# A third buffer for split keys, a second for split queries, weights staged in x's third buffer, and a new order

## The chip, the core and the metric

The kernel runs on one core of a Trainium2 chip. The metric is the device time of one execution in microseconds (us). The engines are TensorE (PE, with its weight loads PEld), VectorE (DVE), ScalarE (ACT), GpSimd (POOL) and SyncE (SP), whose queue issues all the DMAs of this kernel.

## What is computed

An attention with pooled queries feeds a channel mix (inputs: q, k, v of 8 batches, 8 heads, 1152 positions, 64 channels):

```
q_pool = q.reshape(B, H, S // 2, 2, D).mean(axis=3)          # 576 queries
attn   = softmax(scale * q_pool @ k^T)                       # over 1152 keys
x      = (attn @ v), heads side by side                      # (8, 576, 512)
x_prev = x shifted by one position
xk = mu_k * x + (1 - mu_k) * x_prev;  xr = mu_r * x + (1 - mu_r) * x_prev
out = sigmoid(xr @ w_r) * (relu(xk @ w_k)**2 @ w_v)          # 512 -> 1024 -> 512
```

## The kernel before

Everything is 16-bit on PE, in pairs of a high and a low part, so most products are made two or three times. The 64 heads (batch by batch) are gone through in blocks of 96 queries, six a head, 384 in all.

**A block** (function `block`): PE multiplies the nine chunks of keys ks1 with the queries qT (line 544), DVE takes the maximum mx over the chunks (551), PE turns it (554), DVE takes the maximum mb over the partitions (556), PE brings it back as a row (558), ACT writes that row into the low queries (561, qT), PE adds the low parts ks2 with the row (567), and ACT takes the exponentials pf (573). POOL makes their low part pl (581). Three PSUM tiles s are in turn, so up to three blocks are on the way.

**The output** (`window`, `halves`): four or five windows of 128 queries a head (631, 633, 638), and one pair of half windows for two heads (602), summed in the PSUM bank a, divided on DVE, turned (667), and put into xt (678), one of three buffers by batch.

**The feed-forward** (`mix`, `ff`): tiles of 256 rows of x, as soon as a batch is done; all its products stand in line 839, in the PSUM bank f. They fill PE between the blocks of the next batch; what is left over runs after the last block.

**Preparing a head** (`prep`, `queries`): loads of k, v (kr, vr, two buffers each) and of q for two heads (qr, qs, one buffer). Keys are split into high (ACT, line 489) and low (DVE, 492) in kn, **two buffers**. A DMA transpose (499) turns kn into ks1 (two buffers), and a DMA (501) copies its upper half into ks2. The queries of two heads are split in the same way (ACT 441, DVE 445) in qn, **one buffer**, and turned by two DMA transposes (456). So the split of a head's keys waits until the transpose of the head two before has landed, which itself can be issued when PE has done the last scores with that ks1. The heads 0 and 1 are turned on PE (466).

**The weights** (`weights`): 20 pieces of 512 KB are loaded into two staging buffers st (696), decoded from 64-bit numbers by ACT (707 into the bank f, and 716), DVE (719), rounded by ACT (721), with POOL making the low part (722).

**The order**: every operation goes into a list with an engine, a duration, what it reads and writes, and a key (class `Issue`). `run` plays that list through a small model several times (`play`, `follow`), shifts priorities by the numbers in MOVES, and writes the instructions of each engine in the order of the model's start times. Each engine works strictly in that order. LATE, SLACK, SEED and MOVES, and the durations and loads at each `op`, only act through this order.

Of the kernel before, what the change touches and what calls it, by code (L numbers as in the profile page):

```python
# [11 lines left out]
F32 = mybir.dt.float32  # L12
F16 = mybir.dt.float16
BF16 = mybir.dt.bfloat16
I32 = mybir.dt.int32
# [6 lines left out]
P = 128  # L22
# [23 lines left out]
W_FIRST, W_STEP, W_REST, W_REST_STEP = 3.0, 2.0, 32.0, 2.5  # L46
# [3 lines left out]
LATE, SLACK = 0.04, 0.05  # L50
# [6 lines left out]
PE_T = 2  # L57
WDEP = [("ks1", 1), ("ks2", 0), ("vr", 1)]
AHEAD2 = 0
MOVES, BASE, REACH = (  # L60
# [7 lines left out]
SEED, SPREAD = 2, 5.0  # L68


class Issue:
# [15 lines left out]
    def add(self, eng, dur, fn, r=(), w=(), key=0.0, port=None, load=0.0):  # L87
# [23 lines left out]
        self.ops.append((eng, dur, fn, key, deps, eng == "POOL" if port is None else port, None, (dur, load)))  # L111
# [117 lines left out]
    def graph(self, late, slack):  # L229
        ops = self.ops  # L230
        eng = [o[0] for o in ops]
        dur = [o[1] * (1.0 if o[0] in ("PE", "DMA") else 1.0 + late) for o in ops]
        load = [o[7][1] * (1.0 + late) if o[0] == "DMA" else 0.0 for o in ops]
        pred, succ, back = ([[] for _ in ops] for _ in range(3))
        for n, o in enumerate(ops):
            for m, lat in o[4].items():
                more = slack if eng[m] != eng[n] or eng[n] == "DMA" else 0.0
                succ[m].append((n, lat + more))
                pred[n].append(m)
                back[n].append((m, (self.ISSUED + self.LANDED if eng[m] == "DMA" else lat) + more))  # L240
        return (eng, dur, [o[5] for o in ops], load), succ, pred, back
# [54 lines left out]
def kernel(  # L296
# [64 lines left out]
    kn = bufs("kn", 2, [P, NC, P], F16)  # L361
    qn = bufs("qn", 1, [P, 2, NQ, P], F16)
# [15 lines left out]
    sg = bufs("sg", 2, [P, DM], F16)  # L378
# [23 lines left out]
    nc.gpsimd.memset(qn[0][:, 1, :, 0:D], 0.0)  # L402
# [9 lines left out]
    for t_ in xt:  # L412
        nc.vector.memset(t_[:, :, 0:1], 0.0)


    def queries(n, key):

        b, h = divmod(n, H)
        i = n // 2 % 2
# [13 lines left out]
        for j0, j1 in JS:  # L433
            js, jk = slice(j0, j1), range(j0, j1)
            for nj, ck, o_, src in pieces(j0, j1):
                op("DMA", 0.45, lambda o_=o_, src=src: nc.sync.dma_start(o_, src), w=ck,
                   key=key - 2 * NB * PER, load=0.27 * nj + 0.05)
# [3 lines left out]
            op("ACT", (j1 - j0) * P / 1200 + 0.093, lambda js=js, j1=j1, j0=j0: nc.scalar.activation(  # L441
                qn[0][:, 0, js].rearrange("p j (r d) -> p j r d", r=2),
                qs[0][:, js].unsqueeze(2).broadcast_to([P, j1 - j0, 2, D]), AF.Copy, scale=SQ),
               r=[("qs", c) for c in jk], w=[("qn", c) for c in jk], key=key + 1)
            op("DVE", (j1 - j0) * D / 960 + 0.069, lambda js=js: nc.vector.scalar_tensor_tensor(
                qn[0][:, 1, js, D:P], qs[0][:, js], SQ, qn[0][:, 0, js, 0:D], op0=ALU.mult, op1=ALU.subtract),
               r=[("qs", c) for c in jk] + [("qn", c) for c in jk], w=[("qnl", c) for c in jk], key=key + 2, port=True)

        for j0, j1 in JS if n < PE_T else ((0, NQ),):
            js, jk = slice(j0, j1), range(j0, j1)  # L450
            for r_, m, t_, bank, kb, eng in ((0, "qn", "qT", a_b, ("a",), "ACT"), (1, "qnl", "qTl", f_b, ("f",), "DVE")):
                if n < PE_T and j0 < 5:
                    turn16([qn[0][:, r_, c] for c in jk], bank, kb, [(m, c) for c in jk],
                           qT[i][:, r_, js], [(t_, i, c) for c in jk], eng, key + 2)
# [22 lines left out]
    def prep(n, key):  # L477

        b, h = divmod(n, H)
        i, j = n % 2, n % NV  # L480
        def dma(o, src, buf):
            op("DMA", 0.42, lambda: nc.sync.dma_start(o, src), w=[buf], key=key - 2 * NB * PER, load=1.21)
# [3 lines left out]
        for c0, c1 in ((0, 5), (5, NC)):  # L486
            cs = slice(c0, c1)
            nn = (c1 - c0) * D
            op("ACT", nn / 1200 + 0.093, lambda cs=cs: nc.scalar.copy(kn[i][:, cs, 0:D], kr[i][:, cs]),
               r=[("kr", i)], w=[("kn", i, c0)], key=key)  # L490
            e, en, d = ("POOL", nc.gpsimd, nn * 0.0022 + 0.1) if n < KN_POOL else ("DVE", nc.vector, nn / 960 + 0.069)
            op(e, d, lambda cs=cs, en=en: en.tensor_tensor(
                kn[i][:, cs, D:P], kr[i][:, cs], kn[i][:, cs, 0:D], op=ALU.subtract),
               r=[("kr", i), ("kn", i, c0)], w=[("knl", i, c0)], key=key + 1, port=True)
        if n < PE_T:
            turn16([kn[i][:, c] for c in range(NC)], s_b[2], ("s", 2), [(x, i, c) for x in ("kn", "knl") for c in (0, 5)],
                   None, None, (("ACT", 0, 5, ks1[i][:, 0:5], [("ks1", i)]), ("DVE", 5, NC, ks1[i][:, 5:NC], [("ks1", i, 5)])), key + 1)
# [3 lines left out]
        op("DMA", 0.54, lambda: nc.sync.dma_start(ks2[i][D:P], ks1[i][0:D]),  # L501
           r=[("ks1", i), ("ks1", i, 5)], w=[("ks2", i)], key=key + 1, load=0.9)
# [115 lines left out]
    def window(n, w, t):  # L618
# [45 lines left out]
        for t0, t1 in TURN:  # L664
# [7 lines left out]
            for y, (q0, q1) in enumerate(SPAN):  # L672
                if (y < 3) != (t0 == 0):
# [6 lines left out]
                   r=[ka], w=[("xt", b % 3, g, y)], key=t + O_TURN)  # L680


    def weights(n, w, kc, key, step):
        cols = w.shape[1]
        wv = w.bitcast(I32).rearrange("(c p) (f t) -> c p f t", p=P, t=2)
        for c in range(kc):
            for f in range(0, cols, 512):
# [9 lines left out]
                   r=WDEP if iss.nw <= 2 else [], w=[ks], key=key, load=2.41)  # L697
# [5 lines left out]
                mi, km, sz, kz = m_.bitcast(I32), ("em", i), sg[i], ("sg", i)  # L703
# [63 lines left out]
                if dec == "P":  # L767
                    op("ACT", 0.565, lambda sz=sz, wh=wh: nc.scalar.activation(sz, wh.bitcast(F32), AF.Sign),
                       r=[ks], w=[kz], key=key)
                    op("POOL", 1.24, lambda e=e, sz=sz: nc.gpsimd.tensor_tensor(e, e, sz, op=ALU.mult),  # L770
                       r=[ke, kz], w=[ke], key=key)
                else:
                    v_(0.6, lambda ei=ei, wh=wh: nc.vector.scalar_tensor_tensor(
                        ei, wh, -0x80000000, ei, op0=ALU.bitwise_and, op1=ALU.bitwise_or), [ks, ke], [ke])
# [142 lines left out]
    weights("v", w_v, NF, (W_REST + 4 * W_REST_STEP) * PER, W_REST_STEP * PER)  # L917
    tiles = [(t, min(t + T, B * TQ)) for t in range(0, B * TQ, T)]
# [66 lines left out]
```

## Time and profile before

| | |
|---|---|
| median of 3 runs | 1143.21 us (1142.04 to 1145.67) |
| profiled execution | 1141.87 us, span 1140.1 us |
| granted TensorE clock | 1.000 of full speed (2.4 GHz) |
| busy: PE, DVE, ACT, POOL | 1091.6, 921.2, 846.6, 519.5 us |
| chain that ended last | PE 65%, DMA 7%, DVE 3%, ACT 2% |
| of it, by line | L839 26% (bank f), keys' transposes 6%, queries' 2% |

The span runs from the first to the last instruction. Matmul rows are pipelined: each is about 0.2 us long, and the next starts well before its end, so PE's busy time holds more than work. Idle time is shown ahead of the instruction that ended it, with what released it.

### The profile page before, as it was taken

How to read it: one execution, taken by the hardware profiler on the slowest of the kernel's cores; microseconds unless marked ns; L12 is line 12 of the kernel's file. 1: busy time of each engine (PE TensorE's matmuls, PEld its weight loads, DVE VectorE, ACT ScalarE, POOL GpSimd, SP SyncE). 2: the span in 40 equal slices, each digit the busy share in tenths (PEclk: the TensorE clock that was granted, in tenths of full speed). 3: DMA queues.
4: the chain of work that ended last, by engine and by line, in shares of the span. 5: the costliest groups of instructions: out<-in, count | busy, mean ns of one | idle time of the engine just before them, and what ended most of it. 6: DMA issues, size and time to landing. Idle time of an engine off the chain costs nothing.

```text
span 1140.1 us, 44737 instructions
## 1 busy us (share of the span) xinstructions
PE 1091.6 (96%) x18956; PEld 894.1 (78%) x18956; DVE 921.2 (81%) x1860; ACT 846.6 (74%) x1915; POOL 519.5 (46%) x573
## 2 busy tenths in 40 slices
PE   6888899999999999999999999999999999999998
PEld 5777878878787878878786978888787878887565
DVE  8999899988989788789877888797888887874431
ACT  7899987778677786777767676777777686765643
POOL 2566745545454444545353544445353544543111
PEclk9999999999999999999999999999999999999999
DMA  7998576554545555663454553564445534310000
GB/s 204 245 223 186 136 164 126 120 131 98 117 107 125 117 109 116 116 123 80 117 117 79 127 106 96 98 141 107 93 112 107 108 93 86 74 28 11 20 19 28
DMA packets 218745, 125.71 MB, mean 110 GB/s; under 512 B 154032, under 2 KB 190896, under 8 KB 218544
## 3 DMA queue, kind: packets, MB, share of 16 engines
q1 hardware_dynamic: 218544, 122.86, 49.0%
q8 instruction: 148, 2.42, 0.9%
q14 instruction: 53, 0.43, 0.1%
HBM read 67.11 MB, written 9.44 MB: 67 GB/s over the span
## 4 chain that ended last, share of the span: by engine, by line
PE 65%; DMA 7%; DVE 3%; ACT 2%; issue 1%; SPq 0%; ACTq 0%; DVEq 0%
PE f L839 26%; PE s L544 8%; PE s L567 8%; DMA ks<-kn 6%; PE s L839 4%; PE a L638 4%; PE a L633 4%; PE a L631 4%; DMA qT<-qn 2%; PE a L839 2%; PE a L602 1%; PE s L554 1%; PE a L667 1%; PE s L558 1%; DVE mx L551 1%
## 5 line engine op out<-in xcount | busy, mean ns | idle before, releaser
L581 POOL TENSOR_SCALAR pl<-pf 128x864 f16<-128x864 uint16 x384 | 368.8, 960 | 434.3 <-ACT pf L573 404.1
L551 DVE TENSOR_REDUCE mx<-s 128x96 f16<-128x864 f32 x384 | 399.8, 1053 | 84.5 <-PE s L544 55.9
L573 ACT ACTIVATE pf<-s 128x864 int32<-128x864 f32 x384 | 333.6, 883 | 73.6 <-PE s L567 55.6
L544 PE MATMUL s<-qT,ks 128*128 128x96 f16 x3456 | 220.9, 207 | 12.7 <-ACT pf L573 11.4
L567 PE MATMUL s<-qT,ks 128*128 128x96 f16 x3456 | 216.4, 206 | 11.4 <-ACT qT L561 10.6
L544 PEld LDWEIGHTS <-ks 128*128 128x128 f16 x3456 | 183.8, 98 | 40.6 <-issue 16.5
L567 PEld LDWEIGHTS <-ks 128*128 128x128 f16 x3456 | 180.2, 98 | 32.6 <-issue 15.1
L633 PE MATMUL a<-vt,pf 128*128 128x64 f16 x2304 | 192.8, 194 | 0.0
L631 PE MATMUL a<-vt,pf 128*128 128x65 f16 x2304 | 192.4, 193 | 0.3 <-ACT xt L678 0.2
L631 PEld LDWEIGHTS <-pf 128*128 128x128 f16 x2304 | 162.4, 99 | 4.6
L633 PEld LDWEIGHTS <-pf 128*128 128x128 f16 x2304 | 155.6, 97 | 6.3 <-issue 0.5
L561 ACT ACTIVATE qT<-s 1x96 f16<-1x96 f32 x384 | 87.5, 232 | 86.0 <-PE s L558 79.5
L839 PE MATMUL f<-xhk,wk_hi 128*128 128x256 f16 x496 | 135.2, 273 | 0.1
L839 PE MATMUL f<-xhk,wk_lo 128*128 128x256 f16 x496 | 135.2, 273 | 0.0
L839 PE MATMUL f<-xlk,wk_hi 128*128 128x256 f16 x496 | 135.2, 273 | 0.0
L556 DVE TENSOR_REDUCE mb<-s 128x1 f16<-128x128 f32 x384 | 109.4, 287 | 25.6 <-PE s L554 21.7
L638 PE MATMUL a<-vb,pl 128*128 128x65 f16 x2304 | 122.6, 193 | 0.4 <-issue 0.4
L870 POOL TENSOR_TENSOR gl<-g 128x512 f16<-128x512 f32 x72 | 76.5, 1062 | 95.9 <-ACT g L868 93.5
L839 PEld LDWEIGHTS <-wk_hi 128*128 128x128 f16 x1152 | 106.0, 98 | 11.5 <-issue 0.2
L638 PEld LDWEIGHTS <-pl 128*128 128x128 f16 x2304 | 96.7, 98 | 5.5 <-issue 0.5
L839 PE MATMUL f<-wv_hi,g 128*128 128x512 f16 x240 | 90.9, 379 | 0.3 <-ACT em L889 0.3
L839 PE MATMUL f<-wv_lo,g 128*128 128x512 f16 x240 | 90.9, 379 | 0.0
(110 smaller groups left out, 2032.2 us busy)
## 6 DMA issues: line engine op xcount, KB each, us to landing
kr<-in_k_dram SPq DMA_DIRECT2D x64, 288.0 KB
vr<-in_v_dram SPq DMA_DIRECT2D x64, 288.0 KB
qr<-in_q_dram SPq DMA_DIRECT2D x63, 256.0 KB
ks<-ks SPq DMA_DIRECT2D x64, 144.0 KB
out_dram<-em SPq DMA_DIRECT2D x36, 256.0 KB
st<-in_moe_w_k_dram SPq DMA_DIRECT2D x8, 512.0 KB
st<-in_moe_w_v_dram SPq DMA_DIRECT2D x8, 512.0 KB
qr<-in_q_dram SPq DMA_DIRECT2D x32, 64.0 KB
```

The source lines that it names most:

```text
L544: nc.tensor.matmul(cols(c, c + 1), ks1[hp][:, c, :], qhi, start=(c == c0), stop=False, skip_group_check=True)
L551: op("DVE", 0.975, lambda: nc.vector.tensor_reduce(mxz[:, P - QN:P], grid(0, NC).rearrange("p c q -> p q c"), axis=AX.X, op=ALU.max), r=[( ...
L556: op("DVE", 0.199, lambda: nc.vector.tensor_reduce(mbz, s[:, 0:P], axis=AX.X, op=ALU.max), r=[("s", z)], w=[("mb", z)], key=t + O_MAX)
L561: op("ACT", 0.153, lambda: nc.scalar.activation(qlo[0:1], s[0:1, 0:QN], getattr(AF, ROW), scale=1.0 - EPS, alpha=(1.0 + EPS) / (1.0 - EPS) ...
L567: nc.tensor.matmul(cols(c, c + 1), ks2[hp][:, c, :], qlo, start=False, stop=True, skip_group_check=True)
L573: op("ACT", NC * QN / 1200 + 0.06, lambda: nc.scalar.activation(pf[:, :, rows], grid(0, NC), AF.Exp, bias=SHIFT, scale=0.125 / (2.0 * SQ)) ...
L581: op(pe, d, lambda: en.tensor_scalar(pl[:, :, rows], half(pf, U16, 0)[:, :, rows], LO, 1.0, op0=ALU.mult, op1=ALU.mult), r=[("pf", x) for ...
L631: nc.tensor.matmul(bank[:, a0:a0 + VN], half(pf, F16, 1)[:, c, rows], vt[jv][:, c, D:D + VN], start=(w == 1 and c == 0 and hh == 0), stop= ...
L633: nc.tensor.matmul(bank[:, a0:a0 + D], half(pf, F16, 1)[:, c, rows], vt[jv][:, c, 0:D], start=False, stop=False, skip_group_check=True)
L638: nc.tensor.matmul(bank[:, a0:a0 + VN], pl[:, c, rows], vb[jv][:, c, 0:VN], start=False, stop=(c == NC - 1), skip_group_check=True)
L839: nc.tensor.matmul(ps, terms[i][0], terms[i][1], start=(first and i == 0), stop=(i == last), skip_group_check=True)
L870: op("POOL", 2 * n * 0.00203 + 0.08, lambda f2=f2: nc.gpsimd.tensor_tensor(gl[:, f2, 0:n], g32[:, f2, 0:n], gh[:, f2, 0:n], op=ALU.subtrac ...
```

## The change

Keys are split into three buffers (head modulo 3), queries into two. The two staging buffers st and the unused sg are gone; the weights are staged in the two halves of x's third buffer, xt[2], which gets its zero first column on DVE after the decodes, and whose first writes wait for that. The planner's model gets a landing time of its own for each kind of DMA (`more`), other loads, LATE 0.06, and another seed and list of moves.

```diff
-LATE, SLACK = 0.04, 0.05
+LATE, SLACK = 0.06, 0.05
...
+N_KN = 3
+N_QN = 2
+T_MORE = 0.5
...
-    35, 94, 97, 115, 192, 254, 279, 378, 448, 454, 497, 525, 548, 550, 714, 776, 817, 854, 958, 1008, 1035,
...
-), 3000000, 1150.0
-SEED, SPREAD = 2, 5.0
+    1, 3, 25, 41, 42, 69, 101, 158, 269, 371, 436, 439, 580, 670, 676, 689, 702, 1087, 1146, 1213, 1367, 1555,
...
+), 4000000, 1150.0
+SEED, SPREAD = 3, 5.0
...
-            lat = 0.0 if war and e == eng else self.lat(e, eng)
+            lat = self.ops[m][6] if e == "DMA" else 0.0 if war and e == eng else self.lat(e, eng)
...
-    kn = bufs("kn", 2, [P, NC, P], F16)
-    qn = bufs("qn", 1, [P, 2, NQ, P], F16)
+    kn = bufs("kn", N_KN, [P, NC, P], F16)
+    qn = bufs("qn", N_QN, [P, 2, NQ, P], F16)
...
-    st = bufs("st", 2, [P, 1024], I32)
+    st = [xt[2].rearrange("p g t -> p (g t)")[:, z * 1024:(z + 1) * 1024].bitcast(I32) for z in range(2)]
...
-    nc.gpsimd.memset(qn[0][:, 1, :, 0:D], 0.0)
+    for t_ in qn:
+        nc.gpsimd.memset(t_[:, 1, :, 0:D], 0.0)
...
-    for t_ in xt:
+    for t_ in xt[0:2]:
         nc.vector.memset(t_[:, :, 0:1], 0.0)
...
-        i = n // 2 % 2
+        i, u = n // 2 % 2, n // 2 % N_QN
...
-                    qT[i][:, r_, js], qn[0][:, r_, js].rearrange("p j x -> p (j x)")),
-                   r=[(m, c) for c in jk], w=[(t_, i, c) for c in jk], key=key + 2, load=0.155 * (j1 - j0))
+                    qT[i][:, r_, js], qn[u][:, r_, js].rearrange("p j x -> p (j x)")),
+                   r=[(m, u, c) for c in jk], w=[(t_, i, c) for c in jk], key=key + 2, load=0.21 * (j1 - j0), more=T_MORE)
...
-        i, j = n % 2, n % NV
+        i, j, m = n % 2, n % NV, n % N_KN
...
-            op("ACT", nn / 1200 + 0.093, lambda cs=cs: nc.scalar.copy(kn[i][:, cs, 0:D], kr[i][:, cs]),
-               r=[("kr", i)], w=[("kn", i, c0)], key=key)
+            op("ACT", nn / 1200 + 0.093, lambda cs=cs: nc.scalar.copy(kn[m][:, cs, 0:D], kr[i][:, cs]),
+               r=[("kr", i)], w=[("kn", m, c0)], key=key)
...
-            op("DMA", 1.22, lambda: nc.sync.dma_start_transpose(ks1[i], kn[i].rearrange("p c x -> p (c x)")),
-               r=[(x, i, c) for x in ("kn", "knl") for c in (0, 5)], w=[("ks1", i), ("ks1", i, 5)], key=key + 1, load=1.4)
+            op("DMA", 1.22, lambda: nc.sync.dma_start_transpose(ks1[i], kn[m].rearrange("p c x -> p (c x)")),
+               r=[(x, m, c) for x in ("kn", "knl") for c in (0, 5)], w=[("ks1", i), ("ks1", i, 5)], key=key + 1, load=1.9, more=T_MORE)
...
-                   r=[ka], w=[("xt", b % 3, g, y)], key=t + O_TURN)
+                   r=[ka] + ([("xtf",)] if b % 3 == 2 else []), w=[("xt", b % 3, g, y)], key=t + O_TURN)
...
+    op("DVE", 0.07, lambda: nc.vector.memset(xt[2][:, :, 0:1], 0.0), w=[("st", 0), ("st", 1), ("xtf",)]
+       + [("xt", 2, g, 0) for g in range(NG)], key=220.0)
```

What this does to the order is seen best on ACT. Where the same line has another number in the change, it is 4 higher up to the decoding (489 is 493, 707 is 711, 721 is 725) and 2 lower in the feed-forward (815 is 813).

The first place is the keys' split of head 41 (heads are counted from 0), before, with its surroundings; pf are exponentials, one a block, qT the rows, vt the values' split:

```order
L573 ACTIVATE pf_91<-s1_134 128x9x96
L892 ACTIVATE em1_124<-em1_124 128x512
L891 ACTIVATE ex1_122<-ex1_122 128x512
L506 ACTIVATE vt0_85<-vr1_73 128x4x64
L807 ACTIVATE tmp0_119<-xt0_103,omu_r_159 128x256
L807 ACTIVATE tmp1_120<-xt1_104,omu_k_157 128x256
L489 CAST kn1_77<-kr1_71 128x5x64
L489 CAST kn1_77<-kr1_71 128x4x64
L441 ACTIVATE qn0_78<-qs0_75 128x640
L441 ACTIVATE qn0_78<-qs0_75 128x512
L561 ACTIVATE qT0_83<-s2_135 1x96
```

And the split of the same head in the change:

```order
L565 ACTIVATE qT0_85<-s1_132 1x96
L577 ACTIVATE pf_93<-s0_131 128x9x96
L577 ACTIVATE pf_93<-s1_132 128x9x96
L864 ACTIVATE r321_118<-f_135 128x512
L565 ACTIVATE qT0_85<-s2_133 1x96
L682 COPY xt1_106<-a_134 64x64
L682 COPY xt1_106<-a_134 128x256
L866 ACTIVATE g32_0_115<-r321_118 128x512
L493 CAST kn2_78<-kr1_71 128x5x64
L577 ACTIVATE pf_93<-s2_133 128x9x96
L682 COPY xt1_106<-a_134 128x256
L493 CAST kn2_78<-kr1_71 128x4x64
```

Before, 227 exponentials stand ahead of the first of the two instructions, the two follow each other, and the queries' split comes right behind. Now 221 stand ahead of it, an exponential stands between the two, and the buffer is the third one, kn2.

The second place is the end of the weights' decoding on ACT, before; the second row of line 707 is the last read of staged weights into the bank f, and xhk is the first operand of the feed-forward:

```order
L707 ACTIVATE f_137<-st1_126 128x512
L573 ACTIVATE pf_91<-s0_133 128x9x96
L573 ACTIVATE pf_91<-s1_134 128x9x96
L721 CAST wv_hi_129<-ex1_122 128x512
L561 ACTIVATE qT0_83<-s2_135 1x96
L807 ACTIVATE tmp0_119<-xt0_103,omu_k_157 128x256
L707 ACTIVATE f_137<-st0_125 128x512
L573 ACTIVATE pf_91<-s2_135 128x9x96
L716 ACTIVATE em0_123<-st0_125 128x512
L561 ACTIVATE qT0_83<-s0_133 1x96
L815 CAST xhk0_111<-xm1_107 128x256
```

And in the change, where the stage is xt2 and the first row is that last read:

```order
L711 ACTIVATE f_135<-xt2_107 128x512
L565 ACTIVATE qT0_85<-s2_133 1x96
L577 ACTIVATE pf_93<-s1_132 128x9x96
L682 COPY xt0_105<-a_134 128x256
L682 COPY xt0_105<-a_134 64x64
L577 ACTIVATE pf_93<-s2_133 128x9x96
L805 ACTIVATE tmp0_119<-xt0_105,omu_k_155 128x256
L682 COPY xt0_105<-a_134 128x256
L725 CAST wv_hi_127<-ex1_122 128x512
L565 ACTIVATE qT0_85<-s0_131 1x96
L725 CAST wv_hi_127<-ex0_121 128x512
L813 CAST xhk0_113<-xm1_109 128x256
```

The last read into f stands behind 53 exponentials before and behind 49 in the change; on PE, the scores of 57 blocks stand ahead of the first feed-forward product before, and of 53 in the change.

## Rows read from the trace of the kernel before

**Rows 1.** The page: busy us (share of the span) and instructions; then 40 slices, in tenths.

```profile
PE 1091.6 (96%) x18956; PEld 894.1 (78%) x18956; DVE 921.2 (81%) x1860; ACT 846.6 (74%) x1915; POOL 519.5 (46%) x573
...
PE   6888899999999999999999999999999999999998
```

**Rows 2.** Busy time by stage: stretch, its us, busy us (instructions), clock, DMA share, GB/s.

```profile
core 0: us, PE busy (x) PEld busy (x) DVE busy (x) ACT busy (x) POOL busy (x), PEclk, DMA share, GB/s
0.00:133.60 133.60, 106.83 (x2276) 93.69 (x2277) 123.41 (x256) 119.63 (x264) 78.35 (x89) 1.00 0.89 209
30.00:60.00 30.00, 24.27 (x531) 20.95 (x528) 29.31 (x59) 27.03 (x60) 17.75 (x19) 1.00 1.13 250
150.00:1050.00 900.00, 882.01 (x15874) 732.24 (x15873) 753.77 (x1518) 667.83 (x1523) 419.34 (x463) 1.00 0.49 104
1050.00:1140.00 90.00, 86.38 (x543) 52.93 (x541) 29.31 (x59) 44.96 (x98) 12.63 (x12) 1.00 0.07 24
```

**Rows 3.** Instructions with the bank f: ns min/median/max, first and last start us.

```profile
L839 PE MATMUL f<-xhk,wk_hi x496: 269/273/283, 133.6 to 1122.3; 128*128 128x256 f16 x166
...
L707 ACT ACTIVATE f<-st x20: 603/626/674, 24.9 to 130.6; 128x512 f32<-128x512 f32 x20
L719 DVE SCALAR_TENSOR_TENSOR ex<-f,em x20: 676/682/693, 29.7 to 132.8; 128x512 int32<-128x512 int32 x20
```

**Rows 4.** Waits of PE from 150 to 1050 us: us in total, times, longest.

```profile
PE s L567 <- ACT qT L561: 8.8, 10, 1.8
PE s L544 <- ACT pf L573: 3.6, 6, 1.3
```

**Rows 5.** Waits of ACT and of DVE for transposes, 150 to 1050 us.

```profile
ACT kn L489 <- DMA ks<-kn: 30.2, 25, 2.9
...
ACT qn L441 <- DMA qT<-qn: 3.2, 3, 1.5
...
DVE qn L445 <- DMA qT<-qn: 4.2, 2, 2.5
```

**Rows 6.** Busy time in 28 windows over those stalls: two of them, and the sum.

```profile
610.60:616.60 6.00, 4.98 (x45) 2.64 (x44) 3.44 (x8) 2.53 (x8) 0.00 (x0) 1.00 0.93 125
...
826.20:830.90 4.70, 3.48 (x54) 3.15 (x52) 2.76 (x7) 3.02 (x9) 1.46 (x2) 1.00 0.23 51
...
sum 123.50, PE 108.10 PEld 91.55 DVE 84.60 ACT 83.83 POOL 42.25; mean PE 3.86 PEld 3.27 DVE 3.02 ACT 2.99 POOL 1.51
```

**Rows 7.** The chain from 600 to 620 us: start us, us, what.

```profile
602.30 0.38 PE s L544 x9
602.69 0.27 PE a L638 x9
602.96 0.38 PE s L567 x9
...
604.86 0.86 PE f L839 x4
...
608.40 5.08 DMA ks<-kn
...
613.56 0.77 ACT kn L489 x2
...
615.18 0.41 DVE mb L556 x2
...
616.90 0.03 PE a L633
```

**Rows 8.** ACT in order of time from 610 us: start us, us, instruction, [idle before <-releaser].

```profile
610.14 0.50 ACT L807 ACTIVATE tmp<-xt,omu_k 128x256 f32<-128x256 f32 x1
613.56 0.77 ACT L489 CAST kn<-kr 128x320 f16<-128x320 f32 x2 [2.92 <-DMA ks<-kn]
614.36 1.25 ACT L441 ACTIVATE qn<-qs 128x640 f16<-128x640 f32 x2
615.89 0.24 ACT L561 ACTIVATE qT<-s 1x96 f16<-1x96 f32 x1 [0.27 <-PE s L558]
```

**Rows 9.** The start, in order of time: the values' split on DVE, the first scores.

```profile
5.39 0.81 DVE L509 SCALAR_TENSOR_TENSOR vt<-vr,vt 128x256 f16<-128x256 f32 x2
...
9.13 1.60 PE L544 MATMUL s<-qT,ks 128*128 128x96 f16 x18 [0.20 <-ACT qT L471]
```

More of the change, by code (lines that the diff above doesn't have):

```diff
@@ L45 @@
 O_PREP, O_MIX, O_DONE, O_GATE = 10.0, 20.0, -2.0, 1.0
-W_FIRST, W_STEP, W_REST, W_REST_STEP = 3.0, 2.0, 32.0, 2.5
+W_FIRST, W_STEP = 3.0, 2.0
+W_REST = 32.0
+W_REST_STEP = 2.5
 WAIT = {"DVE": 0.1, "ACT": 0.1}
-LATE, SLACK = 0.04, 0.05
+LATE, SLACK = 0.06, 0.05
 KN_POOL, VT_POOL, XL_POOL = 0, 0, 0
@@ L85, in lat, with add @@
         return self.LAT.get((a, b), 0.14 if b == "DMA" else 0.18)
-    def add(self, eng, dur, fn, r=(), w=(), key=0.0, port=None, load=0.0):
+    def add(self, eng, dur, fn, r=(), w=(), key=0.0, port=None, load=0.0, more=0.0):
         n = len(self.ops)
@@ L110, in add @@
                 self.rd.setdefault(b, []).append(n)
-        self.ops.append((eng, dur, fn, key, deps, eng == "POOL" if port is None else port, None, (dur, load)))
+        self.ops.append((eng, dur, fn, key, deps, eng == "POOL" if port is None else port, more, (dur, load)))
     def play(self, p, succ, pred, prio, wait, ahead):
@@ L239, in graph @@
                 pred[n].append(m)
-                back[n].append((m, (self.ISSUED + self.LANDED if eng[m] == "DMA" else lat) + more))
+                back[n].append((m, lat + more + (self.ISSUED + self.LANDED if eng[m] == "DMA" else 0.0)))
         return (eng, dur, [o[5] for o in ops], load), succ, pred, back
@@ L436, in queries @@
                 op("DMA", 0.45, lambda o_=o_, src=src: nc.sync.dma_start(o_, src), w=ck,
-                   key=key - 2 * NB * PER, load=0.27 * nj + 0.05)
+                   key=key - 2 * NB * PER, load=0.25 * nj + 0.05, more=0.2)
             op("DVE", (j1 - j0) * D / 960 + 0.069, lambda js=js: nc.vector.tensor_tensor(
@@ L452, in queries @@
                 if n < PE_T and j0 < 5:
-                    turn16([qn[0][:, r_, c] for c in jk], bank, kb, [(m, c) for c in jk],
+                    turn16([qn[u][:, r_, c] for c in jk], bank, kb, [(m, u, c) for c in jk],
                            qT[i][:, r_, js], [(t_, i, c) for c in jk], eng, key + 2)
@@ L479, in prep @@
         b, h = divmod(n, H)
-        i, j = n % 2, n % NV
+        i, j, m = n % 2, n % NV, n % N_KN
         def dma(o, src, buf):
-            op("DMA", 0.42, lambda: nc.sync.dma_start(o, src), w=[buf], key=key - 2 * NB * PER, load=1.21)
+            op("DMA", 0.42, lambda: nc.sync.dma_start(o, src), w=[buf], key=key - 2 * NB * PER, load=1.0, more=0.15)
         dma(kr[i], k[b, h].rearrange("(p c) d -> p c d", c=NC), ("kr", i))
@@ L488, in prep @@
             nn = (c1 - c0) * D
[L489 to L490 removed]
+            op("ACT", nn / 1200 + 0.093, lambda cs=cs: nc.scalar.copy(kn[m][:, cs, 0:D], kr[i][:, cs]),
+               r=[("kr", i)], w=[("kn", m, c0)], key=key)
             e, en, d = ("POOL", nc.gpsimd, nn * 0.0022 + 0.1) if n < KN_POOL else ("DVE", nc.vector, nn / 960 + 0.069)
             op(e, d, lambda cs=cs, en=en: en.tensor_tensor(
[L493 to L494 removed]
+                kn[m][:, cs, D:P], kr[i][:, cs], kn[m][:, cs, 0:D], op=ALU.subtract),
+               r=[("kr", i), ("kn", m, c0)], w=[("knl", m, c0)], key=key + 1, port=True)
         if n < PE_T:
[L496 removed]
+            turn16([kn[m][:, c] for c in range(NC)], s_b[2], ("s", 2), [(x, m, c) for x in ("kn", "knl") for c in (0, 5)],
                    None, None, (("ACT", 0, 5, ks1[i][:, 0:5], [("ks1", i)]), ("DVE", 5, NC, ks1[i][:, 5:NC], [("ks1", i, 5)])), key + 1)
         else:
[L499 to L500 removed]
+            op("DMA", 1.22, lambda: nc.sync.dma_start_transpose(ks1[i], kn[m].rearrange("p c x -> p (c x)")),
+               r=[(x, m, c) for x in ("kn", "knl") for c in (0, 5)], w=[("ks1", i), ("ks1", i, 5)], key=key + 1, load=1.9, more=T_MORE)
         op("DMA", 0.54, lambda: nc.sync.dma_start(ks2[i][D:P], ks1[i][0:D]),
[L502 removed]
+           r=[("ks1", i), ("ks1", i, 5)], w=[("ks2", i)], key=key + 1, load=0.65, more=0.15)
         for c0, c1 in ((0, 5), (5, NC)):
@@ L696, in weights @@
                 op("DMA", 0.43, lambda s3=s3, src=wv[c, :, f:f + 512]: nc.sync.dma_start(s3, src),
-                   r=WDEP if iss.nw <= 2 else [], w=[ks], key=key, load=2.41)
+                   r=WDEP if iss.nw <= 2 else [], w=[ks], key=key, load=2.2)
                 def v_(dur, fn, r, w, port=True):
@@ L702, in weights @@
                 m_ = em[i]
[L703 removed]
+                mi, km = m_.bitcast(I32), ("em", i)
                 dec = DEC_K if n == "k" else DEC_RV
@@ L766, in weights @@
                         ei, ei, 3, mi, op0=ALU.logical_shift_left, op1=ALU.bitwise_or), [ke, km], [ke])
[L767 to L774, printed above, removed]
+                v_(0.6, lambda ei=ei, wh=wh: nc.vector.scalar_tensor_tensor(
+                    ei, wh, -0x80000000, ei, op0=ALU.bitwise_and, op1=ALU.bitwise_or), [ks, ke], [ke])
                 op("ACT", 0.52, lambda hi=hi, e=e: nc.scalar.copy(hi, e), r=[ke], w=[("w", n, c, f)], key=key)
```

9 lines of the change are left out of this document (4 added, 5 removed), and 9 rows, old and new, of the table AHEAD2.

## The prediction

> **What bounds the kernel now.** I read the busy shares first, then the busy time by stage, then who waits for whom, then the chain. TensorE (PE) is busy 96% of the span [rows 1]; in the stage from 150 to 1050 us it is busy 882.01 of 900 us, and after 1050 us, where only the last feed-forward products are left, 86.38 of 90 us [rows 2]. So there are two places where PE loses time that a change could give back. The first is the start: up to 133.6 us, when the first feed-forward product runs [rows 3], PE is busy 106.83 us while VectorE (DVE) is busy 123.41 and ScalarE (ACT) 119.63 [rows 2]. Attention alone is paced by DVE and ACT, and PE has nothing else to do. The second is the 18.0 us of idle time (900 less 882.01) in the long middle stage. There PE waits mostly for the two ACT steps of a block: the row qT (8.8 us) and the exponentials pf (3.6 us) [rows 4].
>
> Why is ACT late there? It is not short of time: 667.83 of 900 us busy [rows 2]. But it works strictly in order, and its own waits [rows 5] show one that does not belong to the blocks' dependences: 30.2 us, in 25 pieces of up to 2.9 us, at the split of the keys (kn, line 489), until a DMA transpose that still reads the buffer has landed. The same at the queries' split costs ACT 3.2 and DVE 4.2 us. I laid a window over each of these stalls from 150 us on (27 on ACT of over 0.3 us and the two on DVE, of which two share a window), with 3 us behind it: 28 windows, 123.5 us together, hold 15.4 us of PE idle time, of the 18.0 in the whole stage [rows 6]. One seventh of the stage holds six sevenths of the idle time. The chain shows one of them link by link [rows 7]: the transpose is issued at 608.40 and lands 5.08 us later; ACT, free since 610.6, stands 2.92 us [rows 8]; then come the splits of kn, then qn, then the block's row qT at 615.89, and DVE's maximum mb has waited behind the keys' difference as well.
>
> A busy matmul row lasts 0.2 us while the next can start after 0.04, so a wait also eats the tail of the one before it, which the idle time does not count. The Trainium skill (Perfetto Trace Analysis, Identifying the Most-Contended Engine) says that matmul busy time is a bad measure of what TensorE has left, and that the share of weight loading should be taken. By that rule, weight loading runs at 74.1% in the windows (91.55 of 123.5) and at 82.5% in the rest of the stage (640.69 of 776.5) [rows 2, 6], which would make the stalls worth 12.5 us rather than 15.4; the sum below keeps to the idle time.
>
> **The third keys buffer and the second queries buffer.** A split of head n must wait for the transpose of head n-2 before, of head n-3 now. Done at the same place, that would end every one of these waits. But the order has moved the split as well. The transpose that the split of head n waited for is released when PE is through the last scores of head n-4, and now of head n-5, six blocks earlier. And ACT's order now has the split six blocks earlier too: from head 22 on, it stood behind 6(n-3) exponentials less 0 to 2, and now less 5 to 8, mostly 6 or 7. The order takes the buffer for an earlier split, not for a wait that is over sooner. Head 41, whose wait was the longest, shows it: 227 exponentials were ahead of its split, now 221.
>
> What is left is how far behind the transpose's release the split stands. I counted, for heads 22 to 63, the matmuls that PE's order puts between the last scores that release the transpose and the last scores ahead of the split, each at its start-to-start time (0.042 us for a 96-column one, 0.030 for a 65-column one, 0.215 for a 512-column one [rows 7]). It is an estimate: 2.0 us in the mean before, 3.5 us now; under 2 us for 22 of 42 heads before and for 9 now. So ACT arrives some 1.5 us later. If each stall of the ACT queue shrank by 1.5 us, 3.7 of 33.4 us would stay, since few are over 1.5; if the 9 of 22 early ones stayed whole, 13.7 would. I take 8 us, a quarter. The gain is three quarters of 15.4 us: **11.7 us**, between 0 (the stalls stay) and 15.4, plus at most some 4 us for the matmul tails.
>
> **The order at the start.** The weights are decoded into the bank f that the feed-forward also uses, so the first product (133.6 us) comes right behind the last decode step (DVE at 132.8) [rows 3]. PE's order had the scores of 57 blocks ahead of the first product, now 53; ACT's last read of a staged weight stood behind 53 exponentials, now 49. The 20 decodes cost the same. Four blocks thus leave a stage paced by DVE and enter one paced by PE. In the first, DVE's 123.41 us less 20 decode steps of 0.68 make 1.93 us a block over 57 blocks, at 92.4% busy 2.09 us [rows 2, 3]. In the second a block needs 0.38 + 0.38 us of scores, 0.11 for the two small products, and 0.68 for its share of the output (nine windows of 0.80 and one pair of halves of 0.92 in twelve blocks) [rows 7]: 1.55 us. Four times 0.54 is **2.2 us**. Bounds: 0 if the fixed work sets the time after all, 3.2 if a block keeps its 2.34 us (133.6 / 57).
>
> **The first microseconds.** The queries' loads now stand ahead of the values', and DVE adds queries before it splits values (0.81 us). The first scores ran at 9.13 us [rows 9]. Between 0 and 0.81 I take **0.5 us**.
>
> **What I cost at nothing.** The staging in x's third buffer changes no transfer: two halves of 4 KB per partition, as before. It ties x's third buffer to the end of the decodes, but that buffer is first written for batch 2, behind 113 exponentials in ACT's order, and the clearing of its first column stands on DVE right behind the last decode step, at 52 maxima; some 60 blocks cover it, and without them it would cost 0.07 us. The second clearing of queries on POOL (as long as the first, under 0.6 us) now stands ahead of the 16-bit identity; the keys' first transposes need both but wait for the keys' split far longer. The planner's other numbers only act through the order.
>
> **The sum.** 11.7 + 2.2 + 0.5 = 14.4 us. The profiled execution took 1141.87 us, so 1127.5; the median of the runs, 1143.21, lies 1.34 above it: I forecast **1128.8 us**.
>
> **The rivals.** *The stalls go altogether.* The Trainium skill (Perfetto Trace Analysis, Optimization Strategy) says that the same gap coming again and again on the engine that should be full can mean that there are too few buffers for the next tile; by that rule this change is the whole cure. As a mechanism here: no split comes before its transpose has landed, so 15.4 us and the tails of up to 4 us come back, with 2.7 from the start. That is 1143.21 - 18 to 22: 1121 to 1125. For it: PE's idle time hangs on these stalls almost alone. Against it: the split has moved forward by the whole head that the buffer gave.
>
> *The buffer is used up.* The split waits as before, as the bounds above allow; only the 2.7 us at the start come: 1140.5, no change that can be told (0.3% of 1143 us, 3.4 us, is about what a measurement of this kernel can tell from none).
>
> *The weights come too late at the start.* DMA is already full between 30 and 60 us, at a share of 1.13 and 250 GB/s [rows 2]; the order wants the 20 pieces of 512 KB in 49 blocks rather than 53, with the first read behind 3 exponentials rather than 4. A piece takes 2.1 us at 250 GB/s. If half of them come one piece's time late, ACT, which paces this stage with DVE, stands 21 us at its head: 1128.8 + 21 = 1150. It decides from 0.9 us a piece on: then the 14.4 us and 3.4 more are gone. Against it: the first piece was issued long before its read at 24.9 us, and ACT lists no wait for a staged piece at all.
>
> **How the numbers follow.** The forecast case 0.55 (1122 to 1136 by its own terms), the stalls all gone 0.20, the buffer used up 0.14, the late weights or another slip of the order on the slow side 0.11. Faster by over 0.3%: 0.75; within: 0.14; slower: 0.11. The range from 1119 to 1146 leaves out most of the slow case and the end of the good one.
>
> **What would show it.** Right: ACT's wait of kn for its transpose falls from 30.2 to about 8 us, the queries' to under 3; PE's idle time from 150 us on falls from 18 to about 6; the first feed-forward product starts near 125 us. Wrong in the first step: the kn wait stays at 25 pieces, or PE now waits for something else behind the same splits. Wrong in the second: the first product still starts past 131 us, or ACT waits for xt from in_moe_w_k. A new wait of PE or ACT that is longer than 10 us in all and not in [rows 4, 5] would sink the forecast.

## The result, and the profile after

The changed kernel takes **1131.66 us** (median of 4 runs, 1130.02 to 1132.82) against 1144.42 us for the kernel before beside it (4 runs, 1142.04 to 1145.67): 0.989 of the time, 95% interval 0.9866 to 0.9914. It is faster, by 12.8 us; forecast were 14.4 us and 1128.8. The profiled execution took 1132.54 us, with a span of 1130.8 us against 1140.1. The two parts of the forecast fared differently: the middle stage gave more than its term, and the start cost time where it should have given some.

**The middle stage.** Waits from 150 to 1040 us (us in total, times, longest), which answer to [rows 4, 5]:

```profile
ACT kn L493 <- DMA kr<-in_k_dram: 5.2, 4, 1.8
...
ACT kn L493 <- DMA ks<-kn: 2.9, 5, 1.1
...
PE s L562 <- DVE mb L560: 1.8, 5, 0.6
...
PE s L571 <- ACT qT L565: 1.1, 1, 1.1
...
PE s L548 <- ACT pf L577: 0.5, 2, 0.3
```

The keys' split waited 30.2 us for its transposes, in 25 pieces; now 2.9 us in five. The queries' waits (3.2 and 4.2 us) are gone from the list. What ACT waits for at the split now is the load of the raw keys. PE's waits for the row qT and the exponentials fell from 8.8 and 3.6 us to 1.1 and 0.5.

Busy time by stage, with the columns of [rows 2]:

```profile
0.00:134.30 134.30, 101.73 (x2095) 90.85 (x2096) 117.15 (x244) 115.77 (x252) 74.57 (x85) 0.96 0.87 206
150.00:1040.00 890.00, 886.09 (x16021) 739.73 (x16019) 758.15 (x1528) 674.61 (x1535) 424.31 (x469) 1.00 0.50 107
1040.00:1129.00 89.00, 86.70 (x538) 52.46 (x536) 28.02 (x60) 45.77 (x98) 12.46 (x12) 1.00 0.07 24
```

PE is idle for 3.9 us of 890 in the middle; it was 18.0 of 900. The page's chain says the same:

```profile
PE 85%; DVE 3%; ACT 3%; DMA 2%; issue 1%; SPq 0%; DVEq 0%; ACTq 0%
```

PE had 65% and DMA 7% of it.

**The start.** Instructions with the bank f, as in [rows 3]:

```profile
L837 PE MATMUL f<-xhk,wk_hi x496: 269/273/421, 134.3 to 1111.3; 128*128 128x256 f16 x166
...
L711 ACT ACTIVATE f<-xt x20: 600/630/681, 22.7 to 131.2; 128x512 f32<-128x512 f32 x20
L723 DVE SCALAR_TENSOR_TENSOR ex<-f,em x20: 678/684/693, 27.3 to 133.4; 128x512 int32<-128x512 int32 x20
```

The first feed-forward product runs at 134.3 us, not at 125, though only 53 blocks are ahead of it rather than 57. PE is busy 101.73 us up to it (106.83 before), DVE 117.15 (123.41). The clock of PE, 1.00 in this stage before, is 0.96. The first scores, at 9.13 us before [rows 9], come later too:

```profile
9.98 0.88 PE L548 MATMUL s<-qT,ks 128*128 128x96 f16 x9 [1.51 <-ACT qT L475]
```

**The balance.** From its first to its last start, this group of products takes 977.0 us (1111.3 less 134.3) where it took 988.7. The four blocks that moved behind the first product add 6.2 us of PE's work to that stretch (an estimate, four times the prediction's 1.55), so at equal work it is 17.9 us shorter. The start, with the same four blocks counted, is 134.3 + 6.2 - 133.6 = 6.9 us longer. From the last start to the end of the span it is 19.5 us instead of 17.8. Together 17.9 - 6.9 - 1.7 = 9.3 us, the difference of the spans.

The theory to test: the buffers end the waits, but only because the planner's numbers keep the split away from the transpose's release; and the start is dearer by its order. Rivals: the numbers do it without buffers, the buffers do it with any numbers, the searched list does it, and at the start the clock or a loan that is paid back later.

### The profile page after: what moved, and what is told of

Its sections match the earlier page's. It is cut to its first block, busy times and chain, and to the rows that moved or that the text cites. A ratio compares the mean times of both kernels' runs of the same rounds, so it can differ in the third digit from the quotient of the medians.

```text
span 1130.8 us, 44732 instructions
## 1 busy us (share of the span) xinstructions
PE 1089.9 (96%) x18956; PEld 897.3 (79%) x18956; DVE 918.1 (81%) x1860; ACT 849.7 (75%) x1915; POOL 520.4 (46%) x574
## 4 chain that ended last, share of the span: by engine, by line
PE 85%; DVE 3%; ACT 3%; DMA 2%; issue 1%; SPq 0%; DVEq 0%; ACTq 0%
PE f L837 34%; PE s L548 11%; PE s L571 11%; PE a L637 5%; PE a L642 5%; PE a L635 5%; PE s L837 4%; PE a L606 2%; PE s L558 2%; PE a L837 2%; PE a L671 1%; PE s L562 1%; DVE mx L555 1%; ACT pf L577 1%; DMA kr<-in_k_dram 1%
## 5 line engine op out<-in xcount | busy, mean ns | idle before, releaser
L548 PE MATMUL s<-qT,ks 128*128 128x96 f16 x3456 | 221.0, 208 | 12.5 <-ACT pf L577 9.6
```

Of the source, the lines that this page charges most:

```text
L548: nc.tensor.matmul(cols(c, c + 1), ks1[hp][:, c, :], qhi, start=(c == c0), stop=False, skip_group_check=True)
```

## The experiments

In the runs with a written order, the planner is left out and the operations are issued in a given sequence:

```diff
     def run(self, wait, rounds=12):
         ops = self.ops
-        N = len(ops)
...
+        order = struct.unpack(f"<{len(b) // 2}H", b)
...
         for n in order:
             ops[n][2]()
```

Here b is the sequence ORDER, unpacked. Medians and ratios stand against the kernel before in the same job (1142.67, 1142.48 and 1143.41 us in the three jobs). Differences between runs of two jobs mix in the difference of the jobs, which for the kernel before is up to 2 us (1144.42 above and 1142.48 here).

**Buffers alone.** The change's code, ORDER = before's sequence, the clearing of x's third buffer put in behind the last decode step.

> The change's code, with three buffers of split keys, two of split queries and the weights staged in x's third buffer, but every engine's instructions in the order of the kernel before (the clearing of the staged buffer's first column added behind the last decode). Nothing has moved, so a split has a whole head (some 15 us) more until its transpose must have landed. If the waits for transposes were the price, as I say, ACT's wait of kn falls from 30.2 us to under 1, the queries' from 7.4 to 0, TensorE's idle time from 150 us on from 18 us to about 3 to 6, and the time is 1126 to 1130 us, better than the change, since the start stays that of before (first feed-forward product at 133 to 134 us, block 48 at 120 to 121 us). If the waits only hid something else that is late, the time stays above 1138.

Measured: **1124.33 us** (1124.13 to 1129.0), ratio 0.9852 (0.9821 to 0.9883). No wait for a keys' transpose is listed at all; the stage from 150 to 1040 us and the chain:

```profile
150.00:1040.00 890.00, 887.55 (x15968) 738.49 (x15965) 761.88 (x1533) 675.73 (x1546) 422.54 (x465) 1.00 0.49 106
```

```profile
PE 89%; ACT 5%; DVE 4%; issue 2%; DMA 0%; SPq 0%; ACTq 0%; DVEq 0%
```

With the splits at their old places, the buffers alone are worth 18.3 us, and this kernel is faster than both, the change included, and faster than expected. From its first to its last start, the group of products of line 837 (here 1059) takes 969.2 us where it took 988.7 before, with the same blocks ahead: 19.5 us less, of which PE's idle time gave 15.5 (18.0 less 2.5).

**Numbers alone.** The change with the old buffer counts, planned anew.

```diff
-N_KN = 3
-N_QN = 2
+N_KN = 2
+N_QN = 1
```

> The change with two buffers of split keys and one of split queries as before: the planner makes its order anew with the new landing times, loads and moves. In this order the splits stand 2.6 us of TensorE's work behind the release of their transpose in the mean (before 2.0, the change 3.5), and 16 of 42 stand under 2 us (22 and 9). If the third buffer ended the waits in the change, they are back here: kn 25 to 35 us. If the planner's landing times did it, they stay small: 5 to 15 us, and the time lies within 8 us of the change's 1131.7.

Measured: 1144.43 us, ratio 1.0021 (1.0007 to 1.0036). The wait of kn falls to 3.9 us in 7 pieces even so, less than either theory said, and PE's idle time in the middle to 9.0 us, yet no time is gained, where the second theory had it within 8 us of the change: a planner that knows what the transpose takes can place the split late enough with two buffers, and pays for it elsewhere. The group of products shows where:

```profile
L837 PE MATMUL f<-xhk,wk_hi x496: 269/273/421, 131.5 to 1123.2; 128*128 128x256 f16 x166
```

On PE, the scores of 51 blocks stand ahead of the first product, six fewer than before. By the balance used above (six times 1.55 us, an estimate), the stretch from the first to the last start is 6.3 us shorter than before, the start 7.2 us longer and the end 1.6 us longer. So the middle did gain, and the start took it back.

**Buffers with the old numbers.** Three and two buffers, LATE 0.04, no margin for the DMAs (T_MORE 0 and the other landing times out), before's loads; planned anew.

```diff
-LATE, SLACK = 0.06, 0.05
+LATE, SLACK = 0.04, 0.05
...
-T_MORE = 0.5
+T_MORE = 0.0
```

> The change with its three and two buffers, but with the planner's landing times, loads and LATE of before: again an order made anew, with the change's moves. Its splits stand 6 to 9 exponentials ahead of where they stood before, 1.3 us of TensorE's work behind the release in the mean, 29 of 42 under 2 us. If the third buffer ends the waits by itself, kn stays under 5 us. If it is used up by earlier splits and only the landing times keep them apart, the wait is back in full: 30 to 50 us of kn, TensorE idle 18 us or more from 150 us on, and a time of 1140 to 1155 us.

Measured: 1164.33 us, ratio 1.0192 (1.0164 to 1.0221). Its waits in the middle:

```profile
ACT kn L493 <- DMA ks<-kn: 27.1, 23, 3.8
...
PE s L571 <- ACT qT L565: 11.0, 11, 2.2
```

The whole wait is back with a third buffer: 27.1 us in 23 pieces where two buffers had 30.2 in 25. This is the "buffer used up" of the prediction, shown for the wait. The time is worse than that rival's 1140.5 and than the range expected, and PE idles 28.2 us in the middle, so this plan lost more than the buffer. One cause is open: the list of moves in this run, in the numbers alone and in the next run is the one searched for the change, and it shifts another plan here. None of the three was run with the list emptied.

**The margin alone.** The change with T_MORE 0 (the planner's margin for the two kinds of DMA transposes), all else as it is.

```diff
-T_MORE = 0.5
+T_MORE = 0.0
```

> The change's kernel with one number set back: the planner's margin for the two DMA transposes (T_MORE) 0 rather than 0.5; the three and two buffers and the other new numbers stay. The planner then has the split behind the transpose's release by 2.0 us of PE's work in the mean (under 2 us for 23 of 42 heads, as before the change: 2.0, 22; the change 3.5, 9). If the margin is what keeps the order from using up the buffer, the wait of kn for its transpose comes back: 15 to 30 us in some 20 pieces, PE idle 12 to 20 us between 150 and 1040 us, and 1140 to 1148 us. If the buffer by itself ends the waits, under 5 us, as in the change, and 1130 to 1134.

Measured: 1157.82 us, ratio 1.0126 (1.0097 to 1.0154), worse than either theory said. In the middle:

```profile
ACT kn L493 <- DMA ks<-kn: 10.4, 12, 3.4
```

```profile
150.00:1040.00 890.00, 871.73 (x15610) 721.23 (x15607) 763.24 (x1504) 664.21 (x1510) 411.85 (x458) 1.00 0.47 106
```

PE idles 18.3 us there, 14.4 more than in the change, but the kn wait came back only in part. With this list of moves the margin is needed; that it works through this wait alone is not shown, since another number gives another order everywhere.

**Without the search.** The list of moves emptied.

```diff
-MOVES, BASE, REACH = (
-    1, 3, 25, 41, 42, 69, 101, 158, 269, 371, 436, 439, 580, 670, 676, 689, 702, 1087, 1146, 1213, 1367, 1555,
...
+MOVES, BASE, REACH = (), 4000000, 1150.0
```

> The change's kernel with its searched list of moves emptied: the order is the planner's first, by the same numbers (late 0.06, the DMA margin 0.5). The first product is again 53 blocks in. The matmuls between the transpose's release and the split are 4.0 us in the mean, under 2 us for 8 of 42 heads, as in the change (3.5, 9). If the numbers and buffers, not the search, carry the gain in the middle, PE is idle for 3 to 6 us between 150 and 1040 us and the kn wait stays under 5 us; what the time is above 1131.7 then comes from the start and from small gaps: 1132 to 1140. If the search carries it, PE is idle for over 10 us there and the time is over 1140.

Measured: 1131.08 us, ratio 0.9908 (0.9891 to 0.9925), not to be told from the change and a little under the range expected. PE idles 4.9 us in the middle, kn waits 2.3. In sum the searched order carries none of the gain, but it has moved some of it:

```profile
L832 PE MATMUL f<-xhk,wk_hi x496: 269/273/283, 128.6 to 1109.5; 128*128 128x256 f16 x166
```

With the same 53 blocks ahead, the first product runs 5.7 us earlier than in the change (3.8 earlier than in its second profile further down), and the products then take 980.9 us rather than 977.0. By the same balance the start is 1.2 us longer than before and not 6.9. By these single profiles, most of what the change loses at its start goes with the searched list, not with the planner's numbers.

**Each buffer by itself**, in before's order: N_KN 3 and N_QN 1, then N_KN 2 and N_QN 2.

> Before's order word for word, with a third keys buffer and still one queries buffer. With both, this order gave 1124.3. If the keys' buffer is nearly the whole of it, the wait of kn for its transpose is near 0, the waits of the queries' split (7.4 us on ACT and DVE before) stay, PE is idle for 4 to 7 us between 150 and 1040 us, and the time is 1125 to 1129. If the queries' buffer carries as much as its share of the listed waits (7.4 of 37.6 us, so 3 to 4 us of time) 1127 to 1129; if the waits of keys just move to the queries' split, which stands right behind, 1132 to 1138.

> Before's order word for word, with a second queries buffer and still two keys buffers. The wait of kn stays at about 30 us in some 25 pieces, the queries' are gone, PE is idle for 15 to 18 us between 150 and 1040 us, and the time is 1140 to 1143. If the queries' buffer matters as much as the keys', 1132 to 1136.

Measured: 1130.68 us, ratio 0.9904 (0.9887 to 0.9921), and 1140.22 us, ratio 0.9985 (0.9972 to 0.9998). What is left of the waits, in the first and in the second:

```profile
ACT qn L667 <- DMA qT<-qn: 6.8, 5, 3.0
...
DVE qn L671 <- DMA qT<-qn: 2.1, 1, 2.1
```

```profile
ACT kn L715 <- DMA ks<-kn: 30.5, 26, 2.6
...
PE s L793 <- ACT qT L787: 6.6, 10, 1.5
```

The keys' buffer is worth 11.8 us of the 18.3, the queries' 2.3 by itself (barely clear of none) but 6.4 on top of the keys': ACT, let through at kn, reaches the queries' split earlier and waits there instead (6.8 us where it was 3.2). The keys alone came out 1.7 us above the range expected; part of the wait moves.

**Start and rest, crossed.** Before's sequence up to its first feed-forward product, then the change's; and the reverse.

> The change's code with a spliced order: all operations up to the first feed-forward product as the kernel before has them, then the rest in the change's order. The change lost some 8 us at the start (block 48 at 130.4 us, before 120.7) and won some 18 later. If the two are separate, both are had here: block 48 at 120 to 122 us, first feed-forward product at about 134 us, kn's wait under 5 us, and 1122 to 1127 us. If the change's middle rests on its start (the splice leaves what was planned early to come late), the start's gain is lost at the splice, and it is 1130 or more.

> The change's order up to its first feed-forward product, then before's order, with the three and two buffers: the missing fourth of a table (start of before, rest of before 1124.3; start of before, rest of the change 1127.2; start and rest of the change 1131.7). If start and rest add up, 1128.8 (1131.7 less 2.9) within 1.5 us, with block 48 at 129 to 131 us. If the late start is only a loan that the later order gives back, 1124 to 1126.

Measured: 1127.19 us, ratio 0.9867 (0.9841 to 0.9892), and 1130.07 us, ratio 0.9885 (0.9862 to 0.9909). With before's rest, the change's start costs 5.7 us (1130.07 against 1124.33); with the change's own rest 4.5 (1131.66 against 1127.19), or 2.6 by a second measurement of the change further down (1129.75). The medians come from different jobs; by the ratios the three are 3.8, 2.6 and 1.4 us, with intervals that overlap, and the one execution of the buffers alone at a mean clock of 0.995 took 1129.0. So the run times alone do not settle the size. The two traces with the same rest show that nothing is paid back; the buffers alone, then the start of the change:

```profile
L1059 PE MATMUL f<-xhk,wk_hi x496: 269/273/283, 135.4 to 1104.6; 128*128 128x256 f16 x166
```

```profile
L1059 PE MATMUL f<-xhk,wk_hi x496: 269/273/283, 140.1 to 1109.3; 128*128 128x256 f16 x166
```

Both take 969.2 us from first to last; the second begins 4.7 us later and ends 4.7 us later, with 57 blocks ahead in both. In the second the decodes are through long before:

```profile
L945 DVE SCALAR_TENSOR_TENSOR ex<-f,em x20: 675/681/693, 26.7 to 130.6; 128x512 int32<-128x512 int32 x20
```

Its last decode step ends at 131.3 us, where the change's order would begin its products; the four blocks that before's order has first hold them until 140.1, for 8.8 us. And where do the 4.7 us arise? Busy time of the first 30 us in the same two:

```profile
0.00:30.00 30.00, 19.22 (x304) 16.83 (x305) 25.41 (x64) 21.50 (x46) 8.26 (x17) 1.00 0.80 196
```

```profile
0.00:30.00 30.00, 17.62 (x263) 15.60 (x264) 21.93 (x57) 20.33 (x45) 8.28 (x16) 1.00 0.87 211
```

DVE does 124.4 and 124.6 us of work up to the first product, the same, but it is 3.5 us behind after 30 us. DVE in order of time, in the buffers alone and in the start of the change:

```profile
5.04 0.41 DVE L718 TENSOR_TENSOR kn<-kr,kn 128x256 f16<-128x256 f32 x1
5.38 0.83 DVE L735 SCALAR_TENSOR_TENSOR vt<-vr,vt 128x256 f16<-128x256 f32 x2
6.13 0.42 DVE L664 TENSOR_TENSOR qs<-qr 128x256 f32<-128x256 f32 x1
```

```profile
4.97 0.47 DVE L718 TENSOR_TENSOR kn<-kr,kn 128x320 f16<-128x320 f32 x1
5.38 0.27 DVE L664 TENSOR_TENSOR qs<-qr 128x128 f32<-128x128 f32 x1
6.88 0.36 DVE L664 TENSOR_TENSOR qs<-qr 128x192 f32<-128x192 f32 x1 [1.23 <-DMA qr<-in_q_dram]
...
16.88 0.81 DVE L735 SCALAR_TENSOR_TENSOR vt<-vr,vt 128x256 f16<-128x256 f32 x2
```

Before's order split the values while the queries were under way. The change asks for the queries first and has nothing to do until their second piece lands; the values' split comes 11.5 us later, among the first blocks. The exponential of block 6 starts 2.3 us later (31.1 and 28.8 us), that of block 36 3.9 later (98.3 and 94.4) and that of block 48 5.9 later (127.6 and 121.7). So about half of the loss stands by 31 us, and the rest comes after it. The order without the search also splits the values late, at 16.7 us, and has block 6 at 31.1 us too, but block 48 at 124.9.

**Before's first microseconds only.** Before's sequence up to the exponential of block 12, then the change's.

> Before's order up to the exponential of block 12, then the change's, with the three and two buffers. Block 12 was 3.4 us earlier before than in the change (43.4 and 46.8 us). If what the start loses there is lost for good, 1128 to 1129 and block 48 at 127; if blocks 12 to 48 (9.7 less 3.4 us) and not the first ones set the loss, 1130 to 1132 and block 48 at 129 to 131.

Measured: 1135.75 us, ratio 0.9934 (0.9908 to 0.996): neither. The seam made a wait of its own, from 42 to 58 us:

```profile
ACT em L942 <- DMA xt<-in_moe_w_k_dram: 5.1, 2, 3.9
```

The weights come late, as in the prediction's third rival. So this run tells nothing of the first microseconds. It took 4.1 to 6.0 us more than the change with 5.1 us of this wait, but its granted clock was also at half from 48 to 59 us, so the price of the wait by itself is not shown. In the change only 1.2 us of it is listed, for a piece of in_moe_w_v.

**A fuller PE at the start, and the change once more.** At the start of the change the granted clock fell to half three times, and the change's start may be late by that. First, score products repeated (three more in each of the two groups of a block's first scores, six a block):

```diff
-            for c in range(c0, c1):
+            for c in (c0,) * (3 if i < 57 else 0) + tuple(range(c0, c1)):
```

> The change's kernel, with the first score product of each of a block's two groups issued three times more than needed twice (two repeats ahead of the real one, in each group, for the blocks up to 57; the repeats write the same values into the same columns). That is 4 to 6 small products, 0.17 to 0.25 us, a block, while PE has nothing else to do. In the change's trace the granted clock fell to half three times at the start, for 3.4 us each, behind stretches in which PE had been waiting. Theory A: these three stretches make the start late. Then the granted clock is 1.00 in all windows from 0 to 150 us, block 48's exponential comes at 125 to 128 us (130.4 in the change) and the time is 1126 to 1129. Theory B: the start is late by its order (loads, DVE and ACT), and the clock only follows. Then the clock may be 1.00 but block 48 stays within 1.5 us of 130.4 and the time within 2.5 us of 1131.7.

> The change once more, unaltered, for a second profile. If the three stretches at half clock at the start (40, 95 and 132 us, 3.4 us each) belong to this order, they stand within 3 us of the same places; if they are chance, they stand elsewhere or are missing, and block 48 comes 1 to 5 us earlier where they are missing. Time 1131.7 within 1.5 us.

Measured: 1137.34 us, ratio 0.9959 (0.9943 to 0.9975), with block 48 at 134.8 us, and two falls of the clock still; and 1129.75 us, ratio 0.9879 (0.9852 to 0.9907), block 48 at 128.3 us. The repeats neither ended the falls nor brought the blocks forward. They cost 5.7 us (7.6 against the change once more) for 6 x 57 x 0.042 = 14.4 us of PE's work, which shows that PE was not free all through this stage. The block came later than either theory said. In the second profile two of the three falls stand within 3 us of their old places, but the first is elsewhere. Windows around it, the change and then the change again:

```profile
37.50:40.00 2.50, 1.68 (x24) 1.35 (x25) 2.50 (x7) 2.03 (x6) 1.08 (x1) 0.90 1.02 275
40.00:42.50 2.50, 2.50 (x40) 2.50 (x39) 1.80 (x5) 1.13 (x2) 0.16 (x1) 0.50 0.87 286
```

```profile
15.00:17.50 2.50, 1.01 (x12) 0.87 (x13) 2.50 (x7) 2.17 (x5) 0.00 (x0) 0.73 0.85 200
17.50:20.00 2.50, 2.09 (x27) 2.09 (x27) 1.71 (x6) 1.40 (x6) 1.26 (x1) 0.50 0.96 328
```

Block 12, right behind the fall at 40 us, came at 46.8 us in the first and at 44.3 in the second; 2.5 us is about what the later end was too. So, by this one pair, a fall at a bad place may cost some 2.5 us, but the start of the change with one fall (the crossed run, at 40 us) was late as well. With that one fall its last decode step ended at 131.3 us, with three falls in the two profiles of the change at 134.1 and 132.3, so the clock may be 1 to 3 us of the change's start. The order without the search had two falls, and its last decode step ended at 128.5.

## Why the prediction was right, and where it was wrong

- **The time.** 1131.66 us lies 2.9 above the forecast, in its range, and faster was the likeliest sign. It came out near by two errors that cancel in part, which is luck: the middle gave 6.2 us more than its term, the start 9.6 us less than its two terms, and the end of the span 1.7 us less.
- **The buffers: right mechanism, term too small.** "Done at the same place, that would end every one of these waits" is shown by the buffers alone (no kn wait left). "The order takes the buffer for an earlier split" holds for the old numbers (27.1 us) and was taken too far for the new ones: the step that failed is the 8 us left over. 2.9 us were left, and the stage gave 17.9 us where 11.7 was forecast, above the 15.4 of idle time and within the 15.4 + 4 that allowed for the matmuls' tails. In the middle this is the rival in which the stalls go altogether, which was priced at 15.4 to 19.4. The count of splits under 2 us behind the release (9 of 42 in the change) is a rough guide only: the change 9 (2.9 us of wait), without the search 8 (2.3), the old numbers 29 (27.1), but 22 gave 30.2 us before, 23 gave 10.4 without the margin, and 16 only 3.9 with two buffers and new numbers. It made too much of the 9.
- **The two prices of the stalls.** Idle time made them worth 15.4 us, the share of weight loading 12.5; the buffers alone gave 18.3, so idle time was nearer. PE's idle time fell by 15.5 us and the stretch of products by 19.5; the 4 us between are what the prediction allowed for the matmuls' tails, but that they are tails is not shown. The rule of the Trainium skill on a gap that comes again and again (Perfetto Trace Analysis, Optimization Strategy: too few buffers, perhaps) agrees with the runs where the order stays (18.3 us) and not where it is planned anew with the old numbers (27.1 us of wait with three buffers).
- **The order at the start: the price of a block held, the stage did not.** Four times 2.09 us, 8.4, was what four blocks were to take there; in the crossed run they took 8.8, within one execution. What failed is that nothing else in the stage was to change ("the 20 decodes cost the same"): without four blocks it was to end near 125 us, but with 53 blocks and the 20 decodes it ended at 131.3, 132.3 and 134.1 us in the three profiles of this order, and at 128.5 without the search. So the gain on the four blocks was there, and what the stage lost ahead of them outweighed it: in part in the first microseconds, in part by the searched order behind them, and perhaps 1 to 3 us by the clock. How these share it is open. Its premise that PE "has nothing else to do" there fell too: some half of PE's added work showed up in the time.
- **The first microseconds: wrong sign.** 0.5 us was forecast as gained, from 0 to 0.81. Instead the first scores run 0.85 us later, DVE is 3.5 us behind at 30 us in the crossed run, and block 6 is 2.3 us late. The prediction looked at the first scores and priced the values' split as work taken out of the way; it did not ask what DVE would do in its place, and the answer stands in DVE's order: wait for the second piece of the queries. The crossed traces show 4.7 us lost for good over the whole start; what of it this gap makes was not isolated, and the order without the search splits the values as late, with a start only 1.2 us longer than before's.
- **The weights** were not late in the change, as the likeliest case had it.
- **Costed at nothing, and not settled:** staging the weights in x's third buffer is in all runs with before's order, whose last decode step starts at 134.2 to 135.3 us (132.8 before). What of these 1.4 to 2.5 us is the staging's was not tried.

## What to carry to other kernels

A further buffer is worth its wait only as far as the order does not spend it on starting the same work earlier: with a planned order, try it first at the order that exists, and only then plan anew, with a model that knows how long the transfer takes to land. Judge a new order at its start by what each engine does while the first loads are under way, since in this kernel a loss there was carried to the end. And take the idle time around a group of waits for a lower price: here 15.5 us of it ended and 18.3 us were gained.

## What the runs showed of the hardware

The granted clock of TensorE does not hold still from one execution of the same kernel to the next, and a small part of the spread between runs goes with it. Of 35 executions of the kernel before in the three jobs, the three with a mean of 1.000 took 1141.4 us in the mean, and the seven with 0.993 to 0.995 took 1143.9; but those at 0.996 alone go from 1140.8 to 1145.2. The buffers alone took 1124.13 to 1124.44 us in three executions at 1.000 and 1129.0 in one at 0.995. The change took 1128.9 to 1130.0 us at 0.993 and 0.994 in its second job, less than the 1132.5 and 1132.8 at 0.995 in its first, so the mean clock does not order its times. The falls seen go from 2.4 to 1.2 GHz for 3 to 11 us, in the first 135 us. The two shown above stand behind stretches in which PE was busy for less than its full time (1.68 of 2.5 us, and 1.01). The kernel before had such a stretch without a fall in its profile (1.07 of 2.5 us, from 12.5 us), so what sets one off is not settled here.
